# Weights narrowed in 768 columns, their low parts from TensorE, the first batch's attention in float32

## The chip, the cores and the metric

The kernel runs on one core of one Trainium2 chip. The metric is the device time of one execution in microseconds (us), a median over runs. The engines are named as the profile names them: PE is TensorE (PEld its weight loads), DVE is VectorE, ACT is ScalarE, POOL is GpSimd, SP is SyncE, which issues all of this kernel's DMA transfers.

## What is computed

Four batches of 768 tokens go through a gated linear attention (8 heads of 48), a normalised two-layer network with ReLU, and a network with a spatial gate. The weights of the networks but w_sg are float64; everything else is float32.

```
state = alpha[t, :, None] * state + k[t] v[t]^T       # per batch and head, 48 x 48
y[t]  = q[t] state;  x = all heads of y, 384 wide
xn = (x - mean) / sqrt(var + 1e-6) * g_ln
x  = x + relu(xn @ w_ch1) @ w_ch2                     # 384 x 1536, 1536 x 384
h  = gelu(x @ w_in);  u, v = halves of h              # 384 x 1024
vn = (v - mean) / sqrt(var + 1e-6) * g_ln2
vs = w_sg @ vn + b_sg                                 # over tokens, 768 x 768
out = x + (u * vs) @ w_out                            # 512 x 384
```

## The kernel before

Every dense product is made of float16 pairs: an operand is split into a high part (its float16 rounding) and a low part (what is left), and three products (high-high, low-high, high-low) add up in PSUM. `split_path` holds all of it; `general_path` is a fallback that does not run with these inputs.

*Weights.* `w1_piece`, `w2_piece`, `wi_piece` and `wo_piece` each load a block of 384 columns of float64 into one of six `stage` tiles (`stage_load`). `narrow` joins the two 32-bit words of each value to a float32 in three VectorE operations (lines 119, 121, 123). `split_scaled` then scales on ScalarE (L141), rounds to the high part on ScalarE (L142), and subtracts on GpSimd for the low part (L143). w1 and w2 have 12 blocks each, w_in 8, w_out 4. `wg_piece` splits a 128x768 float32 piece of w_sg (L128, L129) and sends it through a DMA transpose.

*Attention.* `att_steps` lists the steps of one chunk of 128 tokens; a batch has 6 chunks, 24 in all. The operands q, k and alpha are transposed, on TensorE with an identity (L256) for chunks 0 to 7, and by DMA later (`halves_of`, `joined`). VectorE scans alpha to running products F and K (L312), multiplies q and k into them (L281); F and K are split into `qs` and `kh` (L351, L364, and GpSimd or VectorE through `low`, L146); `kh` is transposed by DMA to `ks`; ScalarE rescales K (L377); TensorE makes the scores in float32 (`sc`, L385). In chunks 0 to 4 ScalarE copies them out (L401), GpSimd's affine_select zeroes what lies above the diagonal (L402), and ScalarE and GpSimd split the result (L411, L146). The split v (`vs`), `ks` and `ss` then give the state's increment `psd` (L453) and the output `psy` (L467 with the state of the chunks before, L474 within the chunk). `rms_scale` computes 1/sqrt with one Newton step: a power on GpSimd (L213), the rest on VectorE (L211, L215, L216, L219).

*Dense layers.* Two chunks are a group. `A_units` is the first layer (`pg`, L555), whose result is split to `hT` on ScalarE and VectorE (L560, L561); `B_units` the second (L589); `C_units` is w_in (`pgv` L629, `pgu` L654), `D_units` w_sg for a whole batch (L674), `E_units` w_out (L703). A0 is the first layer of group 0, made in halves of 128 tokens; the others take 256 at once.

*Order.* Every step gets a due time from a list of constants (S0, A0 and so on for the first six chunks, C0, R0 and so on for the weights, D0, DS, DX for the dense layers) and they are emitted in that order; a unit of a dense layer also says how many weight pieces must be split before it. From that the program orders the instructions of each engine, and each engine runs its own in that order.

## Time and profile before

| | |
|---|---|
| median of 3 runs | 720.09 us (719.6 to 721.8) |
| profiled execution, first to last instruction (span) | 718.7 us |
| TensorE busy | 632.9 us (88%) |
| VectorE busy | 524.0 us (73%) |
| ScalarE busy | 441.0 us (61%) |
| GpSimd busy | 203.5 us (28%) |
| DMA queue of SP, share of 16 engines' span | 50.2% |

The profile gives one execution; for it the span is the only time recorded. Busy shares are over the whole span and hide that the first 140 us look different from the rest. A line of the profile names the source line, the engine, the operation, what it writes and reads, and how long it was busy.

### The profile page before, as it was taken

Reading aid. Unit: us, or ns where it says so; the run is one execution under the profiler, and the core shown is the slowest. Engines: PE = TensorE matmul, PEld = TensorE weight load, DVE = VectorE, ACT = ScalarE, POOL = GpSimd, SP = SyncE. Lnnn points to the kernel's source line nnn. Section 1 sums busy time; section 2 is a strip of 40 time slices with the busy share of each in tenths; the row PEclk is TensorE's granted clock in tenths of the full one; section 3 lists DMA queues with packets and bytes.
Section 4 is the critical chain, followed back from the end, with each engine's and each line's share of the span. In section 5 each row is a group of like instructions: output and inputs, shape, how many; then the busy total and the mean of one; then the engine's idle time right before and its main releaser. Section 6 shows DMA issues by size and latency. Waiting matters only on the chain. (4 is left out here: it accounts for less than half of the span.)

```text
span 718.7 us, 14699 instructions
## 1 busy us (share of the span) xinstructions
PE 632.9 (88%) x5652; PEld 477.4 (66%) x5652; DVE 524.0 (73%) x1158; ACT 441.0 (61%) x904; POOL 203.5 (28%) x247
## 2 busy tenths in 40 slices
PE   2348889888999998979999997998999989999996
PEld 1237657657576786647676886567676877676784
DVE  3999999978848698466637688577858969433464
ACT  1667667756998649666758639866646557232230
POOL 2657686232613301130404201140403302100000
PEclk9998798999999999999999999999999999999999
DMA  9588867899696216926254207936244232110101
GB/s 216 135 176 190 164 158 196 180 189 149 92 152 111 56 23 127 198 59 121 53 92 92 58 14 134 201 60 118 43 70 56 41 61 48 45 23 12 35 2 71
DMA packets 236575, 72.23 MB, mean 100 GB/s; under 512 B 225872, under 2 KB 232016, under 8 KB 236496
## 3 DMA queue, kind: packets, MB, share of 16 engines
q1 hardware_dynamic: 236496, 71.20, 50.2%
q8 instruction: 46, 0.75, 0.5%
q14 instruction: 33, 0.27, 0.1%
HBM read 35.79 MB, written 4.72 MB: 56 GB/s over the span
## 5 line engine op out<-in xcount | busy, mean ns | idle before, releaser
L555 PE MATMUL pg<-xhT,w1s 128*128 128x256 f16 (+1 forms) x1404 | 156.4, 271 | 13.7 <-DVE hT L561 7.8
L555 PEld LDWEIGHTS <-w1s 128*128 128x128 f16 x1404 | 131.2, 101 | 33.2 <-issue 12.6
L589 PE MATMUL pg<-w2s,hT 128*128 128x384 f16 x864 | 150.5, 333 | 1.8 <-ACT vg L632 1.7
L589 PEld LDWEIGHTS <-hT 128*128 128x128 f16 x864 | 84.9, 99 | 57.8 <-issue 6.4
L674 PE MATMUL pgs<-wgs,vn 128*128 128x256 f16 x864 | 98.2, 275 | 3.4 <-ACT junk L688 2.1
L674 PEld LDWEIGHTS <-vn 128*128 128x128 f16 x864 | 84.9, 99 | 15.1 <-issue 2.3
L146 POOL TENSOR_TENSOR kh<-K,kh 128x512 f16<-128x512 f32 x20 | 24.8, 1241 | 186.8 <-ACT kh L364 126.8
L276 ACT ACTIVATE qksum<-qkT 128x1024 uint16<-128x1024 uint16 x48 | 64.0, 1353 | 12.9 <-DMA qkT<-qk 11.4
L561 DVE SCALAR_TENSOR_TENSOR hT<-pg,hT 128x512 f16<-128x512 f32 (+1 forms) x74 | 49.1, 668 | 30.2 <-ACT hT L560 30.1
L262 ACT ACTIVATE qk<-inp 128x1024 uint16<-128x1024 uint16 x48 | 50.2, 1046 | 26.5 <-DMA qkT<-qk 15.6
L213 POOL TENSOR_TENSOR rr<-ve,consts 128x1 f32<-128x1 f32 x48 | 28.5, 599 | 123.2 <-DVE ve L211 118.8
L629 PE MATMUL pgv<-wis,x2T 128*128 128x512 f16 x216 | 49.7, 379 | 4.2 <-DVE hT L561 2.8
L654 PE MATMUL pgu<-x2T,wis 128*128 128x256 f16 x432 | 49.9, 273 | 3.1 <-DVE hT L561 1.8
L654 PEld LDWEIGHTS <-wis 128*128 128x128 f16 x432 | 41.7, 98 | 10.3 <-DVE hT L561 2.1
L703 PE MATMUL pgo<-wos,uT 128*128 128x384 f16 x288 | 48.0, 326 | 0.0
L560 ACT ACTIVATE hT<-pg 128x512 f16<-128x512 f32 (+1 forms) x74 | 42.0, 578 | 7.6 <-PE pg L555 7.5
L146 POOL TENSOR_TENSOR qs<-F,qs 128x512 f16<-128x512 f32 x22 | 24.9, 1133 | 56.0 <-ACT qs L351 56.0
L703 PEld LDWEIGHTS <-uT 128*128 128x128 f16 x288 | 28.0, 98 | 18.0
L385 PE MATMUL sc<-F,K 48*128 48x128 f32 x352 | 32.5, 313 | 6.9 <-ACT K L377 6.8
L629 PEld LDWEIGHTS <-x2T 128*128 128x128 f16 x216 | 20.5, 98 | 27.1 <-issue 5.1
L442 ACT ACTIVATE junk<-inp 128x384 bf16<-128x384 f32 x72 | 37.1, 519 | 0.8 <-DMA wgs<-wsp 0.7
L385 PEld LDWEIGHTS sc<-F,K 48*128 48x128 f32 x352 | 25.2, 203 | 16.0 <-ACT K L377 9.4
(152 smaller groups left out, 1117.3 us busy)
## 6 DMA issues: line engine op xcount, KB each, us to landing
stage<-in_moe_w_ch_dram SPq DMA_DIRECT2D x24, 384.0 KB, 3.9
inp<-in_alpha_dram SPq DMA_DIRECT2D x24, 192.0 KB, 3.5
inp<-in_q_dram SPq DMA_DIRECT2D x24, 192.0 KB, 3.5
inp<-in_k_dram SPq DMA_DIRECT2D x24, 192.0 KB, 4.2
inp<-in_v_dram SPq DMA_DIRECT2D x24, 192.0 KB, 4.6
out_dram<-x SPq DMA_DIRECT2D x24, 192.0 KB, 2.2
stage<-in_moe_w_in_dram SPq DMA_DIRECT2D x8, 384.0 KB, 3.9
stage<-in_moe_w_sg_dram SPq DMA_DIRECT2D x6, 384.0 KB, 4.6
```

Of the source, the lines that this page charges most:

```text
L146: (nc.vector if on_dve else nc.gpsimd).tensor_tensor(out=out, in0=in0, in1=in1, op=ALU.subtract)
L262: nc.scalar.activation(out=sp, in_=t[:, n].rearrange("p h d -> p (h d)").bitcast(U16) .rearrange("p (x w) -> p w x", w=2), func=AF.Copy)
L276: nc.scalar.activation(out=words[:, :, :, gap:], in_=T[n], func=AF.Copy)
L385: nc.tensor.matmul(out=T["sc", e][:, p, :], lhsT=T["K"][64 * e:64 * e + D, p, :], rhs=T["F"][64 * e:64 * e + D, p, :], start=True, stop=True)
L555: nc.tensor.matmul(out=pg[:, f, :], lhsT=w1s[:, a, kk, ff * P:(ff + 1) * P], rhs=xhT[j][:, r, kk, o], start=(n_ == 0), stop=(n_ == 3 * KD ...
L560: nc.scalar.activation(out=hi, in_=src, func=AF.Relu)
L561: last_dve[0] = nc.vector.scalar_tensor_tensor(out=lo, in0=src, scalar=0.0, in1=hi, op0=ALU.max, op1=ALU.subtract)
L589: nc.tensor.matmul(out=box[s], lhsT=hidden(a, f, s), rhs=w2s[:, r, f, :], start=(f == 0 and a == 0 and r == 0), stop=(f == KF - 1 and r == 1))
L629: nc.tensor.matmul(out=pg, lhsT=x2T[j][:, a, kk, o], rhs=wis[:, r, kk, DG:DI], start=(n_ == 0), stop=(n_ == 3 * KD - 1))
L654: nc.tensor.matmul(out=pg[:, f, :], lhsT=wis[:, a, kk, ff * P:(ff + 1) * P], rhs=x2T[j][:, r, kk, 0:N], start=(n_ == 0), stop=(n_ == 3 * K ...
L674: nc.tensor.matmul(out=pg[:, f, :], lhsT=vn[b * NCH + s][:, a, d * P:(d + 1) * P], rhs=wgs[th][:, r, s, :], start=(n_ == 0), stop=(n_ == 3 ...
L703: nc.tensor.matmul(out=pg, lhsT=gt[key][:, d // 2, a, d % 2, o], rhs=wos[:, r, d, :], start=(d == 0 and a == 0 and r == 0), stop=(d == KG ...
```

## The change

The weights come in pieces of 768 columns (two blocks; w_in in blocks of 256 columns by three rows) into three `stage` tiles of twice the size: 6 pieces each for w1 and w2, 4 for w_in, 3 for w_sg, 2 for w_out. `narrow` takes the three bits of the low word by a ScalarE copy into every other 16-bit word of a `bits` tile, and joins the rest in two VectorE operations. For w1 and w2 the low part comes from TensorE (`split_pe`): a float32 product of the weights with a diagonal of the scale, minus a float16 product of the high part, then a ScalarE copy out of PSUM. w_in and w_out are split on ScalarE and VectorE. Chunks 0 to 5 (`whole`) keep K, the scores and v in float32: no split of F, K, scores and v, K transposed on TensorE, the mask a VectorE product with `causal`, and `psd` and `psy` a third as many products, in float32. The identity and the mask come from a VectorE scan, a float32 product and comparisons. All of `rms_scale` is on GpSimd. In the later chunks `halves_of` and `joined` share one `stage` tile. The due times of the first chunks and of the weights are other numbers.

```
-        t = p2.tile([P, 384], I32, tag="cv", name="cv")
-        nc.vector.tensor_scalar(out=t, in0=hi, scalar1=3, scalar2=-0x40000000, op0=ALU.logical_shift_left,
-                                op1=ALU.bitwise_xor)
-        nc.vector.scalar_tensor_tensor(out=t, in0=lo, scalar=29, in1=t, op0=ALU.logical_shift_right,
-                                       op1=ALU.bitwise_or)
-        nc.vector.scalar_tensor_tensor(out=lo, in0=hi, scalar=-0x80000000, in1=t, op0=ALU.bitwise_and,
-                                       op1=ALU.bitwise_or)
-        return lo.bitcast(F32), lo.bitcast(F32)
+        t = low_bits[0]
+        low_bits.append(low_bits.pop(0))
+        nc.scalar.activation(out=t.bitcast(U16)[:, 0::2], in_=raw.bitcast(U16)[:, :, 1], func=AF.Copy,
+                             scale=2.0 ** -13, bias=-0.5 + 2.0 ** -14)
+        nc.vector.scalar_tensor_tensor(out=lo, in0=hi, scalar=3, in1=t, op0=ALU.logical_shift_left,
+                                       op1=ALU.bitwise_xor)
+        nc.vector.scalar_tensor_tensor(out=lo, in0=hi, scalar=-0x80000000, in1=lo, op0=ALU.bitwise_and,
+                                       op1=ALU.bitwise_or)
+        return lo.bitcast(F32)
+
+    def split_pe(hi, lo, src, scale, diag):
+
+        nc.scalar.activation(out=hi, in_=src, func=AF.Copy, scale=scale)
+        pw = ps.tile([P, 512], F32, tag="g", bufs=3, name="pw")[:, 0:DM]
+        nc.tensor.matmul(out=pw, lhsT=diag, rhs=src, start=True, stop=False)
+        nc.tensor.matmul(out=pw, lhsT=minus, rhs=hi, start=False, stop=True)
+        nc.scalar.activation(out=lo, in_=pw, func=AF.Copy)
...
-        nc.scalar.activation(out=spare, in_=src, func=AF.Copy, scale=scale)
-        nc.scalar.activation(out=hi, in_=spare, func=AF.Copy)
-        nc.gpsimd.tensor_tensor(out=lo, in0=spare, in1=hi, op=ALU.subtract)
...
-        nc.vector.tensor_scalar(out=ve, in0=var, scalar1=EPS / unit, scalar2=None, op0=ALU.add)
...
+        g.tensor_scalar(out=ve, in0=var, scalar1=1.0, scalar2=EPS / unit, op0=ALU.mult, op1=ALU.add)
+        g.tensor_tensor(out=r, in0=ve, in1=nhalf, op=ALU.pow)
+        g.tensor_tensor(out=a, in0=r, in1=ve, op=ALU.mult)
+        g.tensor_tensor(out=a, in0=a, in1=r, op=ALU.mult)
+        g.tensor_scalar(out=a, in0=a, scalar1=-0.5 * c, scalar2=1.5 * c, op0=ALU.mult, op1=ALU.add)
+        g.tensor_tensor(out=r2, in0=a, in1=r, op=ALU.mult)
...
+                for p in range(NP):
+                    nc.tensor.transpose(out=pk[:, p, :], in_=T["K"][:, p, :], identity=ident)
+                nc.scalar.activation(out=T["ks"], in_=pk, func=AF.Copy)
+                T["Kr"] = T["kh"]
...
+                nc.vector.tensor_tensor(out=m, in0=T["sc", e], in1=causal.unsqueeze(1).to_broadcast([P, NP, P]),
+                                        op=ALU.mult)
...
+                    nc.tensor.matmul(out=psd[:, p, :], lhsT=T["ks"][:, p, :],
+                                     rhs=T["vs"][:, 2 * p:2 * p + 2, :].rearrange("p h d -> p (h d)"),
+                                     start=(p == 0), stop=(p == NP - 1), skip_group_check=True)
...
+        nc.vector.tensor_tensor_scan(out=cols, data0=unit, data1=unit, initial=-1.0, op0=ALU.mult, op1=ALU.add)
+        rows = ps.tile([P, P], F32, tag="yd", bufs=1, name="rows")
+        nc.tensor.matmul(out=rows, lhsT=cols[0:1, :], rhs=ones, start=True, stop=True)
+        nc.vector.tensor_tensor(out=ident, in0=rows, in1=cols, op=ALU.is_equal)
+        nc.vector.tensor_tensor(out=causal, in0=rows, in1=cols, op=ALU.is_le)
...
+        trial = p2.tile([P, 2], F32, tag="trial", name="trial")
+        nc.gpsimd.partition_all_reduce(trial[:, 0:1], nhalf, P, ReduceOp.max)
```

GpSimd's order at the start, before: `ident` is the identity, `inp_97` and `inp_98` the two input buffers whose padding is set, ISA a row without a tile.

```order
masks.py:197 MEMSET ident 128x128
L741 MEMSET consts 128x1
L742 MEMSET reset 128x517
L744 MEMSET consts 128x1
masks.py:199 ISA
masks.py:199 AFFINE_SELECT ident<-ident 128x128
L745 MEMSET causal 128x128
L748 MEMSET state 128x384
L750 MEMSET inp_97 128x24x16
L751 MEMSET inp_97 128x8x16
```

And now, the same place up to the trial reduction:

```order
L820 MEMSET inp_94 128x24x16
L821 MEMSET inp_94 128x8x16
L820 MEMSET inp_95 128x24x16
L821 MEMSET inp_95 128x8x16
L837 MEMSET bits 128x768 x2
L839 MEMSET consts 128x1
L840 MEMSET state 128x384
L841 MEMSET reset 128x517
L337 MEMSET K 128x4
L337 MEMSET wk 128x4
L845 ISA
L845 ISA trial<-consts 128x1
```

The padding stands first, the identity is gone, and the trial reduction stands behind all memsets but a short one.

VectorE's order from chunk 0's product with k on, before: `cv` and `stage` are the three operations on a block of weights.

```order
L281 TENSOR_TENSOR K<-pt,K 128x4x128
L119 TENSOR_SCALAR cv<-stage 128x384
L121 SCALAR_TENSOR_TENSOR cv<-stage,cv 128x384
L119 TENSOR_SCALAR cv<-stage 128x384
L123 SCALAR_TENSOR_TENSOR stage<-stage,cv 128x384
L121 SCALAR_TENSOR_TENSOR cv<-stage,cv 128x384
```

And now, with the two masks of chunk 0 (`ss`) among the weights:

```order
L311 TENSOR_TENSOR K<-pt,K 128x4x128
L813 RECIPROCAL g1r<-g1c 128x3
L131 SCALAR_TENSOR_TENSOR stage<-stage,bits 128x768
L133 SCALAR_TENSOR_TENSOR stage<-stage 128x768
L131 SCALAR_TENSOR_TENSOR stage<-stage,bits 128x768
L444 TENSOR_TENSOR ss_248<-sc,causal 128x512
L444 TENSOR_TENSOR ss_249<-sc,causal 128x512
L133 SCALAR_TENSOR_TENSOR stage<-stage 128x768
```

Two wide operations a piece of two blocks stand where three a block stood, and the masks of the first chunks are new on this engine.

TensorE's order just ahead of the first dense product, before: `psy` is the output of chunk 1, `pt` the transposes of chunks 2 and 3, `pg<-xhT,w1s` the first dense product.

```order
L467 LDWEIGHTS wk
L467 MATMUL psy<-sp,wk 128x96
L256 MATMUL pt<-ident,inp_97 128x128 x8
L474 LDWEIGHTS wk
L474 MATMUL psy<-vs,wk 128x48
L256 MATMUL pt<-ident,inp_98 128x128 x4
L555 LDWEIGHTS w1s
L555 MATMUL pg<-xhT,w1s 128x128
```

And now: `psy` is that of chunk 3, `pt` those of chunk 4, `pw` the low part of a block of w2 (the float32 product, then the float16 one).

```order
L283 MATMUL pt<-ident,inp_94 128x128 x4
L141 MATMUL pw<-stage,diags 128x384
L142 LDWEIGHTS minus
L142 MATMUL pw<-w2s,minus 128x384
L530 MATMUL psy<-state,wk 128x96 x4
L536 MATMUL psy<-vs,wk 128x48
L141 MATMUL pw<-stage,diags 128x384
L142 LDWEIGHTS minus
L142 MATMUL pw<-w2s,minus 128x384
L536 MATMUL psy<-vs,wk 128x48 x4
L633 LDWEIGHTS w1s
L633 MATMUL pg<-xhT,w1s 128x128
```

The first dense product moved behind the scores of chunk 3, four chunks' `psd`, and the low parts of 18 of the 24 blocks of w1 and w2; ahead of it stand 56 transposes of operands and 16 of K, where 40 stood before.

## Rows read from the trace of the kernel before

**Rows 1.** Stretches: us, then busy PE, PEld, DVE, ACT, POOL, clock, DMA, GB/s

```profile
0.00:20.00 20.00, 3.95 (x16) 3.00 (x16) 8.99 (x23) 3.86 (x6) 5.33 (x21) 1.00 0.98 225
20.00:99.40 79.40, 53.44 (x548) 43.83 (x549) 78.88 (x163) 53.25 (x123) 54.04 (x56) 0.89 0.72 159
99.40:140.00 40.60, 33.75 (x312) 25.31 (x311) 40.42 (x89) 32.24 (x79) 22.55 (x24) 0.92 0.81 192
140.00:240.00 100.00, 92.73 (x795) 66.93 (x794) 76.48 (x182) 78.64 (x149) 32.24 (x39) 0.98 0.79 132
240.00:600.00 360.00, 336.20 (x3124) 256.28 (x3122) 258.63 (x543) 237.95 (x472) 82.84 (x97) 0.99 0.45 84
```

**Rows 2.** Timeline of the start: start us, us, instruction, idle before and releaser

```profile
3.92 0.55 DVE L444 TENSOR_REDUCE st_in<-inp 128x1 f32<-128x384 f32 x1 [3.92 <-DMA inp<-in_alpha_dram]
...
8.91 0.28 POOL masks.py:199 TENSOR_SCALAR_AFFINE_SELECT ident<-ident 128x128 f32<-128x128 f32 x1 [7.38 <-issue]
...
10.27 1.97 PE L256 MATMUL pt<-ident,inp 128*128 128x128 f32 x8 [10.27 <-POOL inp L751]
10.53 0.19 POOL L751 MEMSET inp<- 128x128 f32 x1
...
11.50 0.42 DVE L312 TENSOR_TENSOR_SCAN F<-pt,consts 128x128 f32<-128x128 f32 x1 [7.02 <-PE pt L256]
```

**Rows 3.** Timeline of TensorE at the first dense products

```profile
53.22 2.34 PE L555 MATMUL pg<-xhT,w1s 128*128 128x128 f16 x20
...
58.79 2.28 PE L555 MATMUL pg<-xhT,w1s 128*128 128x128 f16 x38
```

**Rows 4.** L674's products from 40 to 260 us: ns min/median/max, starts

```profile
L674 PE MATMUL pgs<-wgs,vn x156: 270/273/283, 238.7 to 260.0; 128*128 128x256 f16 x156
```

**Rows 5.** Chain that ended last, 600 us on: start us, us, what

```profile
622.98 11.70 PE pg L589 x72
634.68 11.79 PE pg L555 x108
646.47 3.88 PE pgv L629 x18
650.36 3.93 PE pgu L654 x36
```

**Rows 6.** Timeline of TensorE, a chunk's attention at the fast level

```profile
257.69 1.16 PE L385 MATMUL sc<-F,K 48*128 48x128 f32 x16
...
266.65 0.67 PE L453 MATMUL psd<-vs,ks 128*128 128x96 f16 x12
...
268.28 2.12 PE L555 MATMUL pg<-xhT,w1s 128*128 128x256 f16 x18
```

**Rows 7.** Timeline of TensorE, four transposes among dense products

```profile
163.96 0.60 PE L256 MATMUL pt<-ident,inp 128*128 128x128 f32 x4
```

**Rows 8.** VectorE's lines, 0 to 99.4 us: count, busy us, mean ns, idle

```profile
L121 DVE SCALAR_TENSOR_TENSOR cv<-stage,cv 128x384 int32<-128x384 int32 x24 | 19.3, 816 | 0.1
L123 DVE SCALAR_TENSOR_TENSOR stage<-stage,cv 128x384 int32<-128x384 int32 x24 | 18.5, 776 | 0.0
L119 DVE TENSOR_SCALAR cv<-stage 128x384 int32<-128x384 int32 x24 | 15.6, 651 | 0.1
...
L561 DVE SCALAR_TENSOR_TENSOR hT<-pg,hT 128x384 f16<-128x384 f32 x8 | 4.4, 547 | 0.2 <-ACT hT L560 0.2
```

**Rows 9.** VectorE's lines, 0 to 160 us

```profile
L129 DVE SCALAR_TENSOR_TENSOR wsp<-stage,wsp 128x768 f16<-128x768 f32 x4 | 3.8, 955 | 3.1 <-ACT vn L641 2.6 <-DMA wgs<-wsp 0.5
...
L392 DVE TENSOR_TENSOR sc<-sc,causal 128x512 f32<-128x512 f32 x4 | 2.7, 688 | 0.0
```

**Rows 10.** L121 from 0 to 160 us: ns min/median/max, starts

```profile
L121 DVE SCALAR_TENSOR_TENSOR cv<-stage,cv x32: 518/546/1470, 17.1 to 126.3; 128x384 int32<-128x384 int32 x32
```

**Rows 11.** ScalarE's lines, 0 to 160 us, and the page's costliest groups

```profile
L128 ACT ACTIVATE wsp<-stage 128x768 f16<-128x768 f32 x5 | 4.2, 840 | 6.5 <-DMA wgs<-wsp 5.4 <-DVE ve L211 1.1
...
L276 ACT ACTIVATE qksum<-qkT 128x1024 uint16<-128x1024 uint16 x48 | 64.0, 1353 | 12.9 <-DMA qkT<-qk 11.4
```

**Rows 12.** GpSimd's lines, 0 to 160 us

```profile
L213 POOL TENSOR_TENSOR rr<-ve,consts 128x1 f32<-128x1 f32 x8 | 5.0, 632 | 12.8 <-DVE ve L211 10.8 <-DVE ra L216 2.0
```

More of the change, by code (lines that the diff above doesn't have):

```diff
@@ L6 @@
 from concourse.bass_isa import ReduceOp
-from concourse.masks import make_identity
 F32 = mybir.dt.float32
@@ L349, in _ @@
             scaled("F", "q")
-            work(["qs", "ks", "kh"] if i in (1, 3) else ["qs"], F16)
-            nc.scalar.activation(out=T["qs"][:, 0], in_=T["F"], func=AF.Copy)
+            if whole:
+                work(["ks", "kh"], F16)
+                for n in ("ks", "kh"):
+                    T[n] = T[n].rearrange("p a n t -> p (a n t)").bitcast(F32).rearrange("p (n t) -> p n t", n=NP)
+            else:
+                work(["qs"], F16)
+                nc.scalar.activation(out=T["qs"][:, 0], in_=T["F"], func=AF.Copy)
             if not by_dma:
@@ L422, in _ @@
             masked(1)
-        @step
-        def _():
-            halves(0)
-        @step
-        def _():
-            halves(1)
+        for e in range(0 if whole else 2):
+            @step
+            def _(e=e):
+                halves(e)
         @step
@@ L462, in _ @@
             first = True
+            T["psy"] = psy
+            if whole:
+                for p in range(NP if c else 0):
+                    nc.tensor.matmul(out=psy[:, 2 * p:2 * p + 2, :].rearrange("p h d -> p (h d)"),
+                                     lhsT=T["F"][:, p, :], rhs=state[:, p, :], start=first, stop=False,
+                                     skip_group_check=True)
+                    first = False
+                for h in range(H):
+                    p, e = divmod(h, 2)
+                    nc.tensor.matmul(out=psy[:, h, :], lhsT=T[f"ss{e}"][:, p, :], rhs=T["vs"][:, h, :], start=first,
+                                     stop=(h == H - 1), skip_group_check=True)
+                    first = False
+                return
             if c:
@@ L594, in unit @@
                                                    accum_out=st_xs[:, i:i + 1])
-            units.append((unit, 12 * DM / 2400.0, NW[0] + 4 * part + 4))
+            units.append((unit, 12 * DM / 2400.0, NW[0] + 2 * part + 2))
         return units
@@ L751, in split_path @@
             nc.gpsimd.memset(t[:, 3, :, D:64], 1.0)
+        nc.vector.memset(one, 1.0)
+        cols = p1.tile([P, 2 * U], F32, tag="tm", name="cols")[:, 0:P]
+        ones = p2.tile([P, DG], F32, tag="vg", name="ones")[0:1, 0:P]
+        nc.vector.memset(ones, 1.0)
+        unit = one.to_broadcast([P, P])
+        nc.vector.tensor_tensor_scan(out=cols, data0=unit, data1=unit, initial=-1.0, op0=ALU.mult, op1=ALU.add)
[3 more added lines that the diff above has]
+        nc.vector.tensor_tensor(out=causal, in0=rows, in1=cols, op=ALU.is_le)
+        assert S_SC == S_Q * S_K
+        nc.vector.tensor_scalar(out=minus, in0=ident, scalar1=-1.0, scalar2=None, op0=ALU.mult)
+        for _ in range(2):
+            t = ring.tile([P, KG * U], I32, tag="uT", bufs=3, name="bits")[:, 0:768]
+            nc.gpsimd.memset(t.bitcast(U16)[:, 1::2], 0xC000)
+            low_bits.append(t)
+        nc.gpsimd.memset(nhalf, -0.5)
+        nc.gpsimd.memset(state, 0.0)
+        nc.gpsimd.memset(reset, 0.0)
+        nc.gpsimd.memset(reset[:, 0::P + 1], S_Q)
+        trial = p2.tile([P, 2], F32, tag="trial", name="trial")
+        nc.gpsimd.partition_all_reduce(trial[:, 0:1], nhalf, P, ReduceOp.max)
         load_chunk(0)
```

199 lines of the change are left out of this document (119 added, 80 removed).

## The prediction, made before the changed kernel ran

> **What bounds the kernel now.** I read the stretches first, then the lines of the busiest engine, then the moment from which TensorE has enough to do. The stretches [rows 1] show two regimes. From 20 to 140 us VectorE is busy 119.3 of 120 us and TensorE 87.2: VectorE is the bound there. From 240 to 600 us TensorE is busy 336.2 of 360 and VectorE 258.6; TensorE sets the pace, and idles 6.6%. In the first 20 us nothing is full: the first transposes start at 10.27 us behind the last padding memset, because GpSimd first writes the identity, which it reaches only at 8.91 us after 7.38 us without a release that the profile shows; VectorE's first scan follows at 11.50, although alpha had landed by 3.92 [rows 2]. So what the change is worth is how much earlier TensorE enters its own regime, if the rest stays. Two marks measure that: the first dense product, now at 53.2 us [rows 3], and D0, the first product with w_sg, now at 238.7 us [rows 4]. Between them lie the dense products of the first groups (A0 to A3, B0 to B3, C0 to C2). Behind D0 TensorE's instructions follow one another nearly alike in both orders, so a time won at D0 should reach the end.
>
> **How much work lies between the marks.** At TensorE's fast level A1 to A3 take 11.79 us each, B0 to B3 11.70, C0 to C2 3.88 + 3.93 [rows 5]; A0 is 216 products of 128 columns at 2.28 / 38 = 0.060 us [rows 3], 13.0. That is 13.0 + 35.4 + 46.8 + 23.4 = 118.6 us. Before, the attention of seven chunks (2 to 8) lies there too, each 1.16 for scores and 268.28 - 266.65 = 1.63 for its other products [rows 6], and 14 batches of four transposes at 0.60 [rows 7]: 19.5 + 8.4. Together 146.5 of 185.5 us; 39 us were lost to waits and to the slow level.
>
> **The change, part by part: VectorE up to the first dense product.** By 99.4 us VectorE has narrowed all 24 blocks of w1 and w2 (53.4 us in three operations of 384 columns), scanned chunks 0 to 4, and split the eight hT pieces of A0 (4.4 us) [rows 8]. In the new order VectorE has done the same, one piece and the hT pieces apart, when A0 begins. Eleven pieces of 768 columns need two operations each. The nearest row is the w_sg split, also 768 columns with two sources from SBUF, 0.955 us [rows 9]: 22 x 0.955 = 21.0. The masks of four chunks come to VectorE, 8 x 0.688 = 5.5 [rows 9]. The identity now needs no GpSimd, so the first scan moves from 11.50 to about 5.2 (alpha at 3.92, plus the 1.23 us from first transposes to first scan): -6.3. Sum: 99.4 - 53.4 - 4.4 + 21.0 + 5.5 - 6.3 = 61.8 us if VectorE never waits.
>
> Part of the 53.4 was not VectorE's own: the same 384-column operation took 0.518 us at best and 1.470 at worst [rows 10], in a stretch where GpSimd ran its subtractions. Those of the weights and of the first six chunks go away, so I price the new operations without that stretching. If they were stretched as the old ones were on average (816 over 518 [rows 8, 10], 1.58 times), it would add 12 us; that end is kept. The Trainium skill ("SBUF — State Buffer", Who interferes with whom) says that a VectorE instruction with two SBUF inputs contends with GpSimd instructions that read SBUF. By that rule the 0.955 holds wherever GpSimd is quiet, and the mark stays at 62; without the rule, by the average stretch, it would be 74. The spread of the row agrees with the rule.
>
> ScalarE was busy 57.1 us by 99.4 [rows 1]. It gains one pass of 768 columns a piece: 0.84 by the plain pass, 1.35 by the wide pass over 16-bit words [rows 11]; near the first in width, near the second in strided 16-bit output, so 1.0, 11 us. It loses about five passes of 512 a chunk, estimated at 0.6 from the 0.84: 12 us. So about 56, just below VectorE. Two engines this evenly loaded, in fixed orders, wait for each other, as VectorE in the old order with its surplus never had to.
>
> TensorE gets work it did not have: for each of 18 blocks ahead of A0 a float32 product and a float16 product of 384 columns. No row has a full-height float32 product. The scores bound it: eight of 128 columns take 1.16 [rows 6], 0.145 each, so 0.44 for 384; as their pairs may run side by side on different partitions, up to 0.87. I take the middle, 0.65, plus 11.70 / 72 = 0.16 for float16: 0.82. The other float32 products of a chunk are a third as many as the float16 ones at 2.4 to 4.8 times the time (0.145 or 0.29 against 0.060): 1.3 to 2.6, taken as 2.0. Ahead of A0 then: 18 batches of transposes 10.8, scores 4.6, splits 14.8, the rest 8.0: 38 us at the fast level. At the slow one a 128-column product took 2.34 / 20 = 0.117 us, 1.95 times as long [rows 3], and eight transposes took 1.97 [rows 2]: 71 us in all. The granted clock reads 1.00 in both stretches; the pace of the products at 53 us is that of the 1.2 GHz level, and the pace at 59 us that of 2.4, with the first dense products between. The new order gives TensorE far more to do before them, so I expect the fast level for a good part of the way.
>
> So the first dense product stands between 62 (VectorE never waits) and about 88 (TensorE slow throughout and dear, below). I take 70: VectorE plus an eighth for waits on ScalarE and TensorE.
>
> **From there to D0.** The dense work is the same 118.6. Added: six splits, 4.9. Attention is left for only five chunks: 6 to 8 at 2.79, 8.4; 4 and 5 in float32, 1.16 + 2.0 + 0.60 for K's transposes, 7.5. Ten batches of transposes, 6.0. Sum 145.4. Waits: TensorE idled 6.6% from 240 to 600, 7.3% from 140 to 240, 17% from 99.4 to 140 [rows 1]; 10 to 24 us here. VectorE is left with little of the weights by then, so I take 12. D0 at 70 + 145 + 12 = 227, 11.3 us earlier.
>
> **Edits costed at nothing.** Six GpSimd operations for each inverse root: the power takes 0.63 us [rows 12], a memset 0.19 [rows 2], so the chain is 1.1 to 3.8 us. It is covered by B, 11.7 us, which runs between the v product and D. Without that cover up to 3 us a batch would show, 12 in all. GpSimd's small operations queue ahead of the state's scaling and of the low halves; late next would be the state of the following chunk, and the K that ScalarE rescales behind it. Two more waits of about 7.4 us as the one at 8.91 [rows 2], one ahead of the trial reduction and one ahead of the first root: GpSimd's next work is wanted at about 30 us. Three stage tiles of twice the size hold the same bytes as six; the transfers are the same, and DMA has 28% free from 20 to 99.4 [rows 1]. Chunks 0 to 5 no longer send K through a DMA transpose, which relieves SP's queue.
>
> **The sum.** The profiled execution's span is 718.7 us, 1.4 below the median 720.09 of the three runs. 718.7 - 11.3 = 707.4, plus 1.4: **708.8 us**, range of this case 701 to 717 (first dense product 64 to 77, waits 10 to 14).
>
> **Rivals.** *More is won (chance 0.15).* The engines interleave so well that VectorE never waits: 62 + 145.4 + 10 = 217, 21 earlier, 699; with cheap float32 (0.44) 4 us less, 695. Against it: three engines with 56 to 70 us of work each in a chain.
>
> *TensorE becomes the bound ahead of the first dense product (0.14); slower.* For it: the slow level until 55 us, and 24 blocks of float32 that it never had. Slow and dear, transposes 17.7, scores 9.0, 18 x 1.03 x 1.95 = 36.2, the rest 4 x 2.6 x 1.95 = 20.3: 83 us from 5 us on, so 88; D0 at 88 + 148 + 12 = 248, and 729 us. It decides once the first dense product comes after 81. Against it: work that keeps TensorE this busy is what brought the fast level before. The Trainium skill ("FP8 and Floating Point Precision", TensorE Precision Notes) says that true float32 takes four passes through the array. By that rule the price would be an estimated 4 x 0.16 = 0.65 us, the middle value, and the dear end would fall away; by the scores alone it stays open. No row of this case shows a full-height product.
>
> *It goes elsewhere (0.15).* The dense products then wait for hT's halves on VectorE and ScalarE, which still carry w_in, w_sg and w_out, as they did from 99.4 to 140: 24 us instead of 12, 721, no change. For it: TensorE waited there already; against it: the weight work left then is a third of what it was.
>
> **How the numbers follow.** The forecast has 0.56. The range reaches to 697 (some 0.10 left out below) and to 721 (0.10 of the slower rival above). A measurement tells some 0.3% from nothing, 2 us. Faster: 0.56 + 0.15 + a little of the third, 0.74; within 0.3%: 0.10; slower: 0.16.
>
> **What would show it.** In the new profile: the first scan near 5 us; VectorE's 768-column operations at 0.95; VectorE no longer full after 70 us; the first dense product at 64 to 77; D0 near 227; a float32 split product of 384 columns in 0.44 to 0.87. The prediction is wrong if 128-column products still run at 0.117 us after 70 us, if GpSimd's chain of small operations ends a wait of TensorE, or if the orders behind D0 are paced differently.

## The result, and the profile after

The changed kernel took 703.13 us, the median of four executions, against 720.94 for the kernel before on the same chip: a ratio of 0.973, 95% interval 0.970 to 0.977. One execution, of 3763.94 us, is left out of the ratio; no trace of it exists, and its cause is open. The other three have a median of 702.77, so the gain is 18 us by the medians and 19 by the ratio. The profiled execution has a span of 701.0 us, 17.7 less than before. The page's first part, engines over the whole span:

```profile
PE 650.6 (93%) x5658; PEld 489.4 (70%) x5658; DVE 465.3 (66%) x911; ACT 435.5 (62%) x871; POOL 181.0 (26%) x413
```

TensorE is busy 17.7 us longer than before (650.6 against 632.9) and the span is 17.7 us shorter. So TensorE idles 50.4 us where it idled 85.8. 35.4 us of idle time are gone, and half of them are paid back in work. Where they went is told by the stretches.

First the stretches that answer to [rows 1], then the time up to the first dense product and up to D0; the columns are those of [rows 1].

```profile
0.00:20.00 20.00, 12.77 (x59) 8.97 (x60) 14.90 (x36) 12.45 (x27) 4.56 (x18) 1.00 1.12 228
20.00:99.40 79.40, 73.88 (x630) 55.86 (x629) 68.13 (x143) 55.73 (x120) 12.72 (x31) 1.00 0.85 210
99.40:140.00 40.60, 36.80 (x279) 28.21 (x278) 26.26 (x50) 27.03 (x54) 10.61 (x24) 0.96 0.90 160
140.00:240.00 100.00, 95.98 (x883) 73.07 (x881) 67.17 (x134) 72.51 (x139) 38.23 (x77) 0.98 0.55 92
240.00:600.00 360.00, 335.93 (x3102) 253.60 (x3100) 245.44 (x452) 241.82 (x482) 102.31 (x219) 1.00 0.49 86
0.00:61.63 61.63, 48.88 (x307) 35.60 (x307) 53.82 (x126) 45.21 (x102) 14.47 (x41) 1.00 1.12 237
0.00:223.38 223.38, 202.81 (x1660) 151.06 (x1661) 165.64 (x338) 157.35 (x318) 61.75 (x140) 0.98 0.78 161
```

VectorE is no longer full from 20 to 99.4: 68.1 of 79.4 us, where it had 78.9. TensorE has 73.9 there instead of 53.4, and GpSimd 12.7 instead of 54.0. From 240 to 600 us TensorE's share is as it was. New is the DMA share up to the first dense product: 1.12 at 237 GB/s, where the kernel before had 0.80 at 177. The chain of work from 0 to 70 us now runs through transfers (start us, us, what):

```profile
17.75 5.88 DMA inp<-in_k_dram
...
32.05 5.33 DMA stage<-in_moe_w_ch_dram
...
39.00 5.01 DMA stage<-in_moe_w_ch_dram
```

Whether these transfers are slow or only start late, because their tiles come free late, no run tells apart. That DMA helps to bound the first 60 us of the changed kernel is a rival that none of the experiments tests.

The two marks of the prediction, first from TensorE's timeline (start us, us, instruction), then from the line of the products with w_sg (ns min/median/max, first and last start):

```profile
61.63 4.68 PE L633 MATMUL pg<-xhT,w1s 128*128 128x128 f16 x81
...
66.15 0.90 PE L141 MATMUL pw<-stage,diags 128*128 128x384 f32 x2
66.89 0.32 PE L142 MATMUL pw<-w2s,minus 128*128 128x384 f16 x1
```

```profile
L752 PE MATMUL pgs<-wgs,vn x216: 270/273/282, 223.4 to 249.7; 128*128 128x256 f16 x108
```

The first dense product comes 8.4 us later than in [rows 3], D0 15.3 us earlier than in [rows 4]. A float32 product shows as two records; with its float16 partner it holds TensorE from 66.15 to 67.05, 0.90 us.

VectorE's narrowing, by its lines up to 99.4 us, answers to [rows 8]:

```profile
L131 DVE SCALAR_TENSOR_TENSOR stage<-stage,bits 128x768 int32<-128x768 int32 x16 | 15.6, 972 | 6.0 <-ACT bits L129 5.9
L133 DVE SCALAR_TENSOR_TENSOR stage<-stage 128x768 int32<-128x768 int32 x16 | 15.2, 949 | 0.2
```

That is 32 blocks in 30.8 us, 0.96 a block; before it was 24 in 53.4, 2.24 a block. The new wait, 5.9 us for ScalarE's pass over the low bits, is small beside that.

### The profile page after: what moved, and what is told of

It is laid out like the page before. It is cut to its first block, busy times and chain, and to the rows that moved or that the text cites. A ratio compares the mean times of both kernels' runs of the same rounds, so it can differ in the third digit from the quotient of the medians.

```text
span 701.0 us, 14486 instructions
## 1 busy us (share of the span) xinstructions
PE 650.6 (93%) x5658; PEld 489.4 (70%) x5658; DVE 465.3 (66%) x911; ACT 435.5 (62%) x871; POOL 181.0 (26%) x413
## 3 DMA queue, kind: packets, MB, share of 16 engines
HBM read 35.79 MB, written 4.72 MB: 58 GB/s over the span
## 4 chain that ended last, share of the span: by engine, by line
PE 43%; DVE 17%; ACT 17%; DMA 13%; issue 5%; POOL 3%; SPq 1%; ACTq 0%; DVEq 0%; POOLq 0%
PE pg L667 13%; PE pg L633 9%; PE pgs L752 6%; DMA stage<-stage 4%; PE pgu L732 4%; PE pgv L707 4%; PE pgo L781 3%; ACT stage L306 3%; DMA wgs<-wsp 2%; ACT junk L500 2%; ACT stage L290 2%; DMA inp<-in_alpha_dram 2%; DVE F L345 2%; DVE sc L449 2%; DMA inp<-in_q_dram 2%
## 5 line engine op out<-in xcount | busy, mean ns | idle before, releaser
L633 PE MATMUL pg<-xhT,w1s 128*128 128x256 f16 (+1 forms) x1404 | 151.5, 267 | 13.2 <-DVE hT L639 6.1
L633 PEld LDWEIGHTS <-w1s 128*128 128x128 f16 x1404 | 128.4, 99 | 31.2 <-issue 14.9
L667 PE MATMUL pg<-w2s,hT 128*128 128x384 f16 x864 | 143.7, 326 | 0.3 <-ACT vg L710 0.3
L306 ACT ACTIVATE stage<-stage 128x1024 uint16<-128x1024 uint16 x48 | 64.7, 1354 | 19.1 <-DMA stage<-stage 19.0
L290 ACT ACTIVATE stage<-inp 128x1024 uint16<-128x1024 uint16 x48 | 50.1, 1053 | 30.3 <-DVE K L345 18.4
L150 POOL TENSOR_TENSOR kh<-K,kh 128x512 f16<-128x512 f32 x17 | 20.4, 1199 | 129.2 <-ACT kh L414 129.2
L150 POOL TENSOR_TENSOR qs<-F,qs 128x512 f16<-128x512 f32 x18 | 20.6, 1143 | 79.7 <-ACT qs L386 79.7
L468 ACT ACTIVATE ss<-sc 128x512 f16<-128x512 f32 x36 | 21.1, 596 | 19.0 <-DVE sc L449 19.0
L759 DVE SCALAR_TENSOR_TENSOR pgs<-pgs,g2c,bbc 128x256 f32<-128x256 f32 x48 | 23.4, 487 | 11.3 <-PE pgs L752 10.6
L716 DVE TENSOR_SCALAR vg<-vg,mvv,rv 128x512 f32<-128x512 f32 x24 | 13.8, 579 | 24.4 <-POOL rv L246 23.9
```

The costliest lines, as they stand in the source:

```text
L150: (nc.vector if on_dve else nc.gpsimd).tensor_tensor(out=out, in0=in0, in1=in1, op=ALU.subtract)
L290: nc.scalar.activation(out=sp, in_=t[:, n].rearrange("p h d -> p (h d)").bitcast(U16) .rearrange("p (x w) -> p w x", w=2), func=AF.Copy)
L306: nc.scalar.activation(out=words[:, :, :, gap:], in_=tr, func=AF.Copy)
L633: nc.tensor.matmul(out=pg[:, f, :], lhsT=w1s[:, a, kk, ff * P:(ff + 1) * P], rhs=xhT[j][:, r, kk, o], start=(n_ == 0), stop=(n_ == 3 * KD ...
L667: nc.tensor.matmul(out=box[s], lhsT=hidden(a, f, s), rhs=w2s[:, r, f, :], start=(f == 0 and a == 0 and r == 0), stop=(f == KF - 1 and r == 1))
```

## The experiments

The theory: VectorE was the bound up to 140 us, held by three operations a block and by GpSimd beside it; the change relieves both and starts earlier, and TensorE can afford what it gets. The rivals: the due times are the gain; the roots on GpSimd are; or TensorE has become the bound, so that its low parts cost what the rest wins. All runs are edits of the changed kernel but one. Ratios are against the kernel before on the same chip.

**1. Identity and mask by GpSimd.**

```
-        nc.vector.tensor_tensor(out=ident, in0=rows, in1=cols, op=ALU.is_equal)
-        nc.vector.tensor_tensor(out=causal, in0=rows, in1=cols, op=ALU.is_le)
+        make_identity(nc, ident)
...
+        nc.gpsimd.memset(causal, 1.0)
+        nc.gpsimd.affine_select(out=causal, in_=causal, pattern=[[1, P]], compare_op=ALU.is_ge, fill=0.0,
+                                base=0, channel_multiplier=-1)
```

> The changed kernel, but the identity and the mask are written by GpSimd again, as before; all else as changed. Theory (the early start counts, since VectorE and TensorE are both nearly full from 20 to 62 us): the first scan moves from 5.3 back to about 11.5 us, the first dense product from 61.6 to 66 to 68, and the time rises by 4 to 6 us over the changed kernel, to a ratio of about 0.980 to 0.982 against the kernel before. Rival (the start is hidden behind the first weight transfers, or is caught up before 60 us): the first dense product stays within 2 us of 61.6 and the ratio at 0.973.

Ratio 0.987 (0.985 to 0.989), 1.4% or 10 us above the changed kernel: the theory's direction, twice its size. The timeline of its start says why:

```profile
9.36 0.28 POOL masks.py:199 TENSOR_SCALAR_AFFINE_SELECT ident<-ident 128x128 f32<-128x128 f32 x1 [7.50 <-issue]
...
9.68 3.04 DVE L829 TENSOR_SCALAR minus<-ident 128x128 f16<-128x128 f32 x1 [8.75 <-POOL ident masks.py:199]
9.70 1.97 PE L285 MATMUL pt<-ident,inp 128*128 128x128 f32 x8 [9.70 <-POOL ident masks.py:199]
...
9.82 2.96 DVE L848 TENSOR_SCALAR diags<-ident 128x128 f32<-128x128 f32 x1
9.90 1.82 POOL L832 MEMSET bits<- 128x768 uint16 x2
...
13.16 0.41 DVE L344 TENSOR_TENSOR_SCAN F<-pt,consts 128x128 f32<-128x128 f32 x1
```

The first scan comes 7.9 us late, not 6.2: two VectorE operations on the identity now stand beside a row of GpSimd's memsets and take 3 us each, ending as the row ends. In the changed kernel they stand beside fewer memsets and take 1.01 and 0.95 us, and three more of 128 columns take 0.68 together with GpSimd quiet:

```profile
2.60 1.01 DVE L834 TENSOR_SCALAR minus<-ident 128x128 f16<-128x128 f32 x1
2.74 0.95 DVE L853 TENSOR_SCALAR diags<-ident 128x128 f32<-128x128 f32 x1
...
8.86 0.68 DVE L851 TENSOR_SCALAR diags<-ident,g1c 128x128 f32<-128x128 f32 x3
```

The Trainium skill ("SBUF — State Buffer", Who interferes with whom) says that a tensor_scalar in VectorE's two-port mode and GpSimd lock each other out for a whole instruction; the trace agrees that VectorE is held up, 3.04 against 1.01 and 0.23 us, but 3.04 is longer than any one of these memsets, and that the operations ran in that mode no run shows.

**2. The inverse roots as before** (power on GpSimd, the rest on VectorE).

```
-        g.tensor_scalar(out=ve, in0=var, scalar1=1.0, scalar2=EPS / unit, op0=ALU.mult, op1=ALU.add)
+        nc.vector.tensor_scalar(out=ve, in0=var, scalar1=EPS / unit, scalar2=None, op0=ALU.add)
...
```

> The changed kernel with the inverse roots as before: the power on GpSimd, the four other small operations on VectorE. Theory (both homes are off the path): within 2 us of the changed kernel, ratio 0.971 to 0.976. Rival A (moving them to GpSimd freed VectorE and gave the gain that I had not forecast behind the first batch): 3 to 6 us slower, ratio about 0.978 to 0.981. Rival B (the GpSimd chain of six, on which VectorE waits 23.9 us in all for the v scale, costs time): 2 to 5 us faster, ratio about 0.967 to 0.970.

Ratio 0.975 (0.972 to 0.978), not told apart from 0.973. Either home will do, and both rivals fall, although the page of the changed kernel has VectorE idle behind this chain:

```profile
L716 DVE TENSOR_SCALAR vg<-vg,mvv,rv 128x512 f32<-128x512 f32 x24 | 13.8, 579 | 24.4 <-POOL rv L246 23.9
```

Those 23.9 us are idle time of an engine that has it to spare; TensorE's waits do not name the chain.

**3. The old due times**, one line of numbers.

```
-LATE, TC, D0, DS, DX, KQ, NE, KA, LD, S0, A0, S1, A1, S2, A2, S3, A3, S4, A4, S5, A5, C0, R0, C1, R1, C2, R2, C3, R3, MB, MD, QB, HB, KV, KG_, KW, KW2 = 16.42, 19.13, 24, 0.88, 1.18, 8.0, 4.0, 8.0, 5.66, 0.8, 16, 13, 12, 28, 14, 38, 14, 46, 14, 54, 14, 2, 3, 18, 3, 36, 3, 60, 5, 224.0, 96.0, 0.0, 96.0, 19.0, 0.0, 10.0, 0.0
+LATE, TC, D0, DS, DX, KQ, NE, KA, LD, S0, A0, S1, A1, S2, A2, S3, A3, S4, A4, S5, A5, C0, R0, C1, R1, C2, R2, C3, R3, MB, MD, QB, HB, KV, KG_, KW, KW2 = 16.42, 19.13, 34.67, 0.88, 1.18, 8.0, 4.0, 8.0, 5.66, 0.81, 23.56, 12.81, 17.01, 14.01, 20.14, 18.48, 37.52, 44.88, 16.36, 54.38, 5.73, 6.53, 2.0, 22.41, 2.02, 52.23, 1.0, 76.35, 1.24, 224.0, 96.0, 0.0, 96.0, 19.0, 0.0, 10.0, 0.0
```

> The changed kernel with the due times of the kernel before (the one line of numbers), so the same instructions in another order. Theory (the gain is work taken off VectorE and GpSimd, the numbers only fit the order to it): at least half of the 19 us stays; first dense product at 62 to 70 us, 701 to 711 us, ratio 0.973 to 0.987. Rival (the order is the gain): ratio 0.993 or more, 716 us or more, first dense product after 72.

Ratio 0.979 (0.977 to 0.981): about 4 us of the 19 are the new numbers', with intervals that almost touch. The first dense product came at 74.6, past the bound that I had set for the rival, and the time hardly followed. That was the first sign that this mark sets nothing.

**4 and 5. The low parts of w1 and w2 from VectorE, or from GpSimd**, in place of the two products.

```
-        nc.scalar.activation(out=hi, in_=src, func=AF.Copy, scale=scale)
-        pw = ps.tile([P, 512], F32, tag="g", bufs=3, name="pw")[:, 0:DM]
-        nc.tensor.matmul(out=pw, lhsT=diag, rhs=src, start=True, stop=False)
-        nc.tensor.matmul(out=pw, lhsT=minus, rhs=hi, start=False, stop=True)
-        nc.scalar.activation(out=lo, in_=pw, func=AF.Copy)
+        split2(hi, lo, src, scale)
```

`split2` makes the high part on ScalarE and the low part in one VectorE operation. Run 5 puts these in place of the same lines:

```
+        spare = p2.tile([P, DM], F32, tag="spare", name="spare")
+        nc.scalar.activation(out=spare, in_=src, func=AF.Copy, scale=scale)
+        nc.scalar.activation(out=hi, in_=spare, func=AF.Copy)
+        nc.gpsimd.tensor_tensor(out=lo, in0=spare, in1=hi, op=ALU.subtract)
```

> The changed kernel, but the low parts of w1 and w2 come from VectorE (one operation of 384 columns with the scale, out of SBUF, a block) and the two products and the ScalarE copy are gone. About 18 of 24 blocks lie ahead of the first dense product. Theory as predicted (VectorE is the bound there): 18 x 0.55 = 10 us more on VectorE, first dense product at about 70, 6 to 10 us slower than the changed kernel, ratio 0.981 to 0.987. Rival (TensorE, relieved of about 18 x 0.9 = 16 us, was the bound ahead of the first dense product, or ScalarE): first dense product at 56 to 61, as fast or faster, ratio 0.965 to 0.973.

> The changed kernel, but the low parts of w1 and w2 come from GpSimd as before the change: ScalarE writes the scaled float32 and the high part, GpSimd subtracts; the two products a block and the copy out of PSUM are gone, so ScalarE has as many passes as with them, VectorE as many, and TensorE about 24 x 0.9 = 22 us less. Theory (VectorE is the bound up to about 100 us, and it is slowed where GpSimd reads two operands): VectorE's 768-column operations rise from 0.96 to 1.2 to 1.5 us, and the time is 3 to 8 us above the changed kernel, ratio 0.978 to 0.985. Rival (GpSimd beside VectorE costs nothing, and what TensorE is spared counts): the operations stay at 0.96, ratio 0.960 to 0.972.

Run 4: 0.988 (0.984 to 0.991), about 10 us slower than the changed kernel; run 5: 0.975 (0.972 to 0.979), not told apart from it. Both have the first dense product at 37.9, 24 us earlier, and D0 no earlier (228.3 and 223.1). So run 4 has the size that its theory gave, but not by its way, a first dense product at 70; and in run 5 VectorE's wide operations rose to 1.02 and 1.08 us on average, not to 1.2 to 1.5. Part of the 24 us is order: the program puts the scores of two chunks ahead of that product here, and of four in the changed kernel. Run 5's stretches show what TensorE does with the room, first in run 5, then in the changed kernel:

```profile
70.00:80.00 10.00, 6.54 (x42) 4.02 (x40) 7.34 (x12) 8.15 (x14) 7.60 (x10) 1.00 0.91 226
80.00:110.00 30.00, 25.41 (x146) 21.89 (x146) 23.68 (x52) 16.15 (x38) 3.23 (x9) 0.60 1.02 221
```

```profile
80.00:110.00 30.00, 30.00 (x246) 23.30 (x245) 18.76 (x35) 14.75 (x29) 1.21 (x1) 1.00 0.74 178
```

It runs dry from 70 to 80, and from 80 to 110 it is granted 0.60: mostly the 1.2 GHz level, where the changed kernel had 1.00 and 246 products instead of 146.

**6. A GpSimd subtraction added for each block of w1 and w2**, its result unused.

```
+        spare = p2.tile([P, DM], F16, tag="spare", name="spare")
+        nc.gpsimd.tensor_tensor(out=spare, in0=src, in1=hi, op=ALU.subtract)
```

> The changed kernel with one GpSimd subtraction of 384 columns added to each of the 24 blocks of w1 and w2, whose result nothing reads: some 24 us of GpSimd work, nothing else changed. GpSimd is busy 9.1 of 40 us from 20 to 60, so it has room. Theory (VectorE is slowed by it): VectorE's 768-column operations rise above 1.1 us and the time by 3 to 8 us, ratio 0.978 to 0.985. Rival (no contention worth the name; the gain came from the operations that VectorE no longer has): operations at 0.96, the time within 2 us of the changed kernel, ratio 0.970 to 0.976.

Ratio 0.982 (0.980 to 0.985), 6 us slower, as the theory had it; but the means stayed below its 1.1 us: L131 rose from 0.97 to 1.05, L133 from 0.95 to 1.08. The form is in the spread (ns min/median/max), first the changed kernel's, then this one's:

```profile
L133 DVE SCALAR_TENSOR_TENSOR stage<-stage x16: 929/950/962, 13.4 to 93.3; 128x768 int32<-128x768 int32 x16
```

```profile
L133 DVE SCALAR_TENSOR_TENSOR stage<-stage x15: 933/959/1728, 13.5 to 96.5; 128x768 int32<-128x768 int32 x15
```

Most operations are untouched and a few lose up to 0.78 us, most of the 0.92 us that one of the added operations takes. That is some 3 us of VectorE's time in all. The added work also holds the piece's `stage` tile longer, and TensorE's products up to D0, the same number, took 5.6 us longer at a granted clock of 0.96 instead of 0.98; how the 6 us divide stays open.

**7. The float32 product twice.**

```
+        nc.tensor.matmul(out=pw, lhsT=diag, rhs=src, start=True, stop=True)
         nc.tensor.matmul(out=pw, lhsT=diag, rhs=src, start=True, stop=False)
```

> The changed kernel with the float32 product of each of the 24 blocks of w1 and w2 made twice (the second overwrites the first): 24 x 0.75 = 18 us more on TensorE, nothing else. Theory (by 20 to 60 us TensorE, 34.5 of 40, is close behind VectorE, 37.5 of 40, and behind that it is the bound): the idle 5.5 us take a part, 10 to 16 us slower than the changed kernel, ratio 0.987 to 0.996. Rival (TensorE has slack under VectorE until 100 us): less than 4 us, ratio below 0.979.

Ratio 0.998 (0.995 to 1.001): 18 us, nearly the whole gain and more than the theory's 10 to 16, eaten by 24 products. TensorE's timeline has them back to back, 0.68 us apart:

```profile
50.72 0.84 PE L141 MATMUL pw<-stage,diags 128*128 128x384 f32 x2
51.40 0.84 PE L142 MATMUL pw<-stage,diags 128*128 128x384 f32 x2
52.08 0.32 PE L143 MATMUL pw<-w2s,minus 128*128 128x384 f16 x1
```

Those are 16.3 us of work, and D0 came 19.0 us later, though the first dense product came at 58.7, 3.0 us earlier, as the order has fewer chunks ahead of it. 18 of the 24 added products stand ahead of it all the same. A microsecond added to TensorE costs at least one here, and added work is not free ahead of the dense products either.

**8 and 10. The first batch's attention in float16 again**, with the new and with the old due times (the line of run 3).

```
-    NF = NCH
+    NF = 0
...
-                work(["qs"], F16)
+                work(["qs", "ks", "kh"] if i in (1, 3) else ["qs"], F16)
```

> The changed kernel with the attention of the first batch in float16 halves as before the change (F, K, scores and v split, K through a DMA transpose, mask by GpSimd in chunks 0 to 4, three products for one); weights, identity and roots as changed, the negated identity in another tile. It takes some 5 ScalarE passes and 5 GpSimd operations of 512 columns a chunk back, and spares TensorE the float32 products. Theory (ScalarE and GpSimd are then the load that VectorE waits for): 4 to 12 us slower than the changed kernel, ratio 0.979 to 0.990. Rival (float32 on TensorE costs more than the splits did): as fast or faster, ratio below 0.974.

> The changed kernel with the first batch's attention in float16 halves and also the due times of the kernel before, that is, the changed weights, identity and roots without the float32 attention, in the order that the float16 attention was tuned with. Theory (the float16 attention costs by its work on ScalarE and GpSimd): TensorE idles at least 40 us ahead of the first product with w_sg, time 715 to 728 us, ratio 0.992 to 1.008. Rival (the 25 us of the float16 attention were due times that did not fit it): ratio 0.985 or less.

Ratios 1.009 (1.006 to 1.012) and 0.993 (0.991 to 0.996). Run 8 lies far outside both of its ranges, some 25 us slower than the changed kernel; run 10 has the time of its theory, but TensorE idles 35.8 us, not 40. Part of run 8's loss is the order, as run 10 is 1.5% better. What stays is not the order: without the float32 attention and with the old due times the rest of the change wins 5 us. Run 8 from 20 to 60 us:

```profile
20.00:60.00 40.00, 30.32 (x189) 18.03 (x188) 31.16 (x62) 36.00 (x82) 21.27 (x29) 0.87 0.98 230
```

ScalarE is the full engine here, 36.0 of 40, and VectorE, 31.2, waits.

**9. w1's low parts from TensorE, w2's from GpSimd.**

```
-                        split_pe(hi[:, n], lo[:, n], w[:, n], scale, diags[0][:, KD])
+                        split_pool(hi[:, n], lo[:, n], w[:, n], scale)
```

> The changed kernel with the low parts of w1 from TensorE as changed and those of w2 from GpSimd as before the change. TensorE is spared about 12 x 0.9 = 11 us, GpSimd gets 12 x 1.0 = 12 us, both mostly from 40 to 75 us, where TensorE has just become full. Theory (a us of TensorE's work ahead of the first product with w_sg counts in full, as twice the float32 product showed, and GpSimd alone with half of the blocks slows VectorE little): first product with w_sg at 215 to 221, 4 to 8 us faster than the changed kernel, ratio 0.962 to 0.968. Rival (VectorE and ScalarE are as full as TensorE, so what TensorE is spared turns into waits, as with all low parts on GpSimd): first product with w_sg at 222 to 226, within 3 us of the changed kernel, ratio 0.970 to 0.977.

A miss on both sides: 0.982 (0.979 to 0.986), 6 us slower. The first dense product moved to 44.0, with three chunks' scores ahead of it, and then it went as in runs 4 and 5, with 24.05 busy of 30 us from 80 to 110 at a granted clock of 0.54.

**11. The kernel before with the float32 attention alone**: its `att_steps` is that of the changed kernel, but for `halves_of` and `joined`.

```
+    NF = NCH
...
+        whole = i < NF
```

> The kernel before with the float32 attention of the first batch alone (chunks 0 to 5 as in the changed kernel); weights, identity, roots and due times as before. It takes from GpSimd the masks and the splits of these chunks, from ScalarE some 5 passes a chunk, and adds 8 masks to VectorE by 99 us. Theory (VectorE's narrowing was stretched by GpSimd's work and stays the bound with three operations a block): the 384-column operations fall from 0.65 to 0.82 to about 0.55 to 0.65 us, TensorE's idle time ahead of the first product with w_sg falls from 56 to 40 to 50 us, 4 to 14 us faster than the kernel before, ratio 0.981 to 0.994. Rival A (the float32 attention is the whole gain): ratio 0.978 or less. Rival B (VectorE's own three operations bound it, so nothing comes of it alone): ratio 0.996 to 1.004.

Ratio 0.987 (0.984 to 0.989), 9.5 us faster: the theory. VectorE's lines up to 99.4 us:

```profile
L122 DVE SCALAR_TENSOR_TENSOR cv<-stage,cv 128x384 int32<-128x384 int32 x29 | 21.3, 752 | 0.1
L124 DVE SCALAR_TENSOR_TENSOR stage<-stage,cv 128x384 int32<-128x384 int32 x29 | 18.3, 646 | 0.1
L120 DVE TENSOR_SCALAR cv<-stage 128x384 int32<-128x384 int32 x29 | 11.4, 407 | 0.1
```

The same three operations fall from 2.24 us a block [rows 8] to 1.81 (752 + 646 + 407 ns), and 29 blocks are done where 24 were. Nothing of the weights' code is changed here: what left is work beside them, above all GpSimd's, while VectorE stayed full:

```profile
20.00:99.40 79.40, 61.94 (x518) 52.92 (x517) 78.80 (x189) 47.68 (x118) 33.92 (x38) 0.96 0.71 178
```

**12. Only the last three pieces of w2 from VectorE**, the six blocks whose products stand behind the first dense product.

```
-                if on_pe:
+                if on_pe and i < 3:
```

> The changed kernel, but the low parts of the last three pieces of w2 (of six) come from VectorE, one operation of 768 columns each, with one ScalarE pass; the six pairs of products and the six copies out of PSUM are gone. These pairs stand behind the first dense product, from 66 to 83 us, where TensorE of the changed kernel is busy all of the time (29.4 of 29.4 us from 70 to 99) and VectorE is not (21.5 of 29.4). Theory (what counts there is TensorE's own work, as doubling the float32 products showed): 6 x 0.9 = 5.4 us less on TensorE, 2 to 5 us faster than the changed kernel, ratio 0.966 to 0.970, first product with w_sg at 218 to 221. Rival (fewer products let TensorE idle there, and the granted clock falls as in the runs with the low parts elsewhere): TensorE idles more than 24 us ahead of the first product with w_sg, and the time is the changed kernel's or more, ratio 0.973 or above.

Ratio 0.964 (0.962 to 0.965), 697.66 us: faster than the changed kernel by about 1%, more than the theory's range; by the spans, 697.3 against 701.0, it is 3.7 us. The stretches of run 5, in this run:

```profile
70.00:80.00 10.00, 10.00 (x129) 8.35 (x127) 10.00 (x17) 8.85 (x18) 3.13 (x7) 1.00 0.69 213
80.00:110.00 30.00, 27.83 (x212) 20.94 (x211) 16.70 (x31) 13.56 (x31) 0.83 (x1) 1.00 1.04 186
```

The first dense product stays at 61.3, with the same chunks ahead of it, and TensorE keeps the 2.4 GHz level.

**Together.** TensorE's busy and idle time from the start to D0, from the stretches, with the granted clock:

| kernel | D0 | busy | idle | clock | span less D0 |
|---|---|---|---|---|---|
| before | 238.7 | 182.5 | 56.1 | 0.94 | 480.0 |
| changed | 223.4 | 202.8 | 20.6 | 0.98 | 477.6 |
| 1 identity by GpSimd | 232.4 | 204.1 | 28.3 | 0.98 | 479.5 |
| 2 roots on VectorE | 226.4 | 205.0 | 21.4 | 0.98 | 477.5 |
| 3 old due times | 226.2 | 202.0 | 24.2 | 0.98 | 480.3 |
| 4 low parts on VectorE | 228.3 | 199.4 | 28.9 | 0.94 | 479.8 |
| 5 low parts on GpSimd | 223.1 | 196.3 | 26.7 | 0.93 | 481.6 |
| 6 GpSimd load added | 232.4 | 208.4 | 24.1 | 0.96 | 477.5 |
| 7 float32 twice | 242.4 | 222.6 | 19.8 | 0.96 | 479.5 |
| 8 float16 attention | 248.0 | 201.1 | 46.9 | 0.94 | 477.7 |
| 9 w2 on GpSimd | 230.2 | 203.4 | 26.8 | 0.93 | 478.7 |
| 10 float16, old due times | 240.4 | 204.5 | 35.8 | 0.92 | 478.7 |
| 11 before, float32 attention | 237.5 | 192.5 | 45.0 | 0.96 | 475.3 |
| 12 last of w2 on VectorE | 219.9 | 198.1 | 21.9 | 0.98 | 477.4 |

The last column spreads by 6 us and D0 by 28: most of what is won or lost is decided by D0. Run 11 is the exception: against the trace of the kernel before its D0 is 1.2 us earlier and 4.7 us lie behind it. The traces are of single executions on several chips, on which the median of the kernel before ran from 720.9 to 724.3 us, so differences of 2 or 3 us between rows say little.

TensorE's instructions up to D0, counted in the first column of brackets, show what the runs without the pairs save: run 5, then run 12.

```profile
0.00:223.07 223.07, 196.34 (x1588) 155.45 (x1589) 169.97 (x338) 157.88 (x318) 86.37 (x164) 0.93 0.77 161
```

```profile
0.00:219.93 219.93, 198.08 (x1643) 149.78 (x1644) 168.71 (x342) 154.55 (x309) 59.61 (x140) 0.98 0.85 164
```

The changed kernel has 1660. Run 5 makes the same products but for the 24 pairs (72 records) of 0.84 us (0.68 + 0.16), 20.2 us of work; yet TensorE is busy only 6.5 us less. The other products took 13.7 us longer. By the same sum they took 16.8 longer in run 4 and 10.7 in run 9, and 0.3 in run 12. In the first three the granted clock fell after TensorE had run dry; in run 12, which keeps the order, it did not. So the last six pairs cost most of their length (TensorE's busy time falls by 4.7 of 5.0 us, D0 by 3.5), and taking away all 24 gains nothing. That the first 18 pay for themselves by keeping the clock up is likely, but not shown: in runs 4, 5 and 9 the order changed as well, and no run took the early pairs away in the order of the changed kernel.

## Why the prediction was right, and where it was not

The forecast was 708.8 us, 701 to 717 for its own case; the measured 703.1 lies in that case. The way there was not as told: the first dense product came at 61.6, outside its 64 to 77, and the later waits were 7.8 us, below its 10 to 14. Both would have given a shorter time, and an underestimate of TensorE's work by 8.5 us made up for most of it. That the time came out so near is in part luck. Point by point:

- **VectorE's work.** 768-column operations forecast at 0.955, measured 0.949 and 0.972; masks at 0.688, measured 0.681; first scan at 5.2, measured 5.28. That GpSimd's work is what stretches such operations is shown by runs 6 and 11.
- **Start.** Sized at 6.3 us; run 1 lost 10, as its VectorE operations on the identity met GpSimd's memsets.
- **TensorE's new work.** The float32 product, taken at 0.65 between 0.44 and 0.87, takes 0.68. The estimate by the Trainium skill ("FP8 and Floating Point Precision", TensorE Precision Notes), also 0.65, agrees. Up to the first dense product TensorE was busy 48.9 us; I had 38 at the fast level and 71 at the slow one. Eight transposes took 2.23 us at 4.16; four took 0.62 at 17.89, so the fast level came by then. What was mis-sized is the other float32 products of a chunk, taken as 2.0 between 1.3 and 2.6: they take 3.5, by the rows below this list. Four chunks ahead of the first dense product make that 6 us more than the sum had, and the two behind it make 3 of the 8.5 us of the next point.
- **From the first dense product to D0.** 145.4 us of work and 12 of waits from a mark at 70. Measured: 61.6, then 202.8 - 48.9 = 153.9 of work and 7.8 of waits. Three errors, -8.4, +8.5 and -4.2, make D0 come at 223.4 instead of 227; the first two cancel.
- **The step that failed.** "VectorE, then the first dense product, then the work from there" took that product for the mark that sets D0. It does not. It came at 37.9 in runs 4 and 5, at 61.6 in the changed kernel and at 74.6 in run 3, and D0 at 228.3, 223.1, 223.4 and 226.2; in run 7 it came 3.0 us earlier and D0 19.0 later. One reason is that it is not the same point in every order: two, four or five chunks' scores stand ahead of it (runs 4 and 5, the changed kernel, run 3). In runs 4 and 5 the dense products start early, and then TensorE waits or runs at the slow level. TensorE's work and waits have to be added up all the way to D0; that sum only books the time, and what brings the waits about has to be read from the runs. That the first dense product fell on 61.6, close to my 61.8 without waits, is no proof of that sum: VectorE was busy only 53.8 of those 61.6 us.
- **Edits costed at nothing.** The roots: right (run 2). The waits of 7.4 us ahead of the trial reduction and the first root did not come: the reduction ran at 4.72 right behind the memsets. DMA, which I had with 28% free, was at 1.12 up to 61.6 us. Behind D0 the changed kernel gained 2.4 us more, which no run explains; the last column of the table spreads by more than that.
- **Signs.** Of those that were to show it, the first dense product missed its range. Of those that would have made it wrong, none came: a 128-column product took 0.058 us (4.68 / 81) from 61.6 on, and GpSimd's chain ended no wait of TensorE.
- **Rivals.** More is won: its mark, 62, and its short waits came, but the work came out 8.5 us above its sum, so 699 was not reached. TensorE as the bound: not at the slow level and not slower, but run 7 shows that it is one; 24 more products and the kernel is no faster than before. It goes elsewhere: the later waits were 7.8 us, not 24.

The other float32 products of one chunk in the changed kernel, from each start to the next 0.86, 0.94 and 1.74 us:

```profile
43.34 1.02 PE L512 MATMUL psd<-vs,ks 128*128 128x96 f32 x8
44.20 0.33 PE L142 MATMUL pw<-w1s,minus 128*128 128x384 f16 x1
...
45.65 1.10 PE L530 MATMUL psy<-state,F 128*128 128x96 f32 x8 [0.53 <-ACT x L591]
46.59 1.91 PE L536 MATMUL psy<-vs,ss 128*128 128x48 f32 x16
48.33 0.62 PE L283 MATMUL pt<-ident,inp 128*128 128x128 f32 x4
```

How the 19 us divide: four kernels with the old due times can be set side by side. The float32 attention alone wins 9.5 us (run 11), the rest of the change alone 5 (run 10), both together 15 (run 3), so within the noise the two add up; the new due times bring the other 4. Taking single parts out of the finished kernel does not give these sizes: without the early identity it loses 10 us (run 1), without the float32 attention 25 (run 8), part of it because the new due times do not fit that kernel (run 10).
